# Sliding-window attention ahead of two expert layers: two-bank score tiles, one maximum per chunk and a shorter list of weight conversions

## The chip, the cores and the metric

The program runs on one core of a Trainium2 chip. The metric is the device time of one execution in microseconds (us); the profile's own clock starts with the first instruction (the span). The engines are called TensorE (PE in the rows, its weight loads PEld), VectorE (DVE), ScalarE (ACT), GpSimd (POOL) and SyncE (SP, which only issues DMAs).

## The reference

```python
scores = (1 / sqrt(64)) * q @ k.T            # 4 batches, 8 heads, 576 positions, head size 64
scores = where(0 <= i - j < 64, scores, -1e9)
attn = softmax(scores); x = attn @ v         # x: 2304 tokens x 512
logits = x @ w_gate                          # 8 experts
# every (token, expert) pair in falling order of its logit: give the token to the expert
# if the token has none yet and the expert has fewer than 288
out[e's tokens] = relu(x[e's tokens] @ w1[e]) @ w2[e]        # 512 -> 1024 -> 512
h = out @ w_in; y = maximum(0.01 * h, h) @ w_out             # 512 -> 2048 -> 512
```

## The kernel before

There are three stages in one program, and each engine works its own list of instructions in the order of the program text.

**Attention** (`attention`, lines 58 to 223) handles 18 chunks of 128 queries, two windows of 64 each; a query looks at two windows of keys. For chunk c, `scores` writes a mask and then 32 small matmuls into score tiles; VectorE takes the maximum per query and head (line 131) and multiplies it by -0.125 (line 133); `exps` makes four exponentials on ScalarE for either half a of the heads (line 139), with that number as bias. `trans` turns the probabilities with eight matmuls into the PSUM tile "apt", and ScalarE copies each half out (line 146). `values` makes 32 matmuls into the tile "ao"; VectorE adds up, inverts, forms the logits (the values carry eight more columns for them) and scales the rows (line 169, tile "ax"), which a DMA writes to "xd". The loop runs one chunk ahead for scores and two behind for values: scores(i), exps(i,0), values(i-2), trans(i-1), exps(i,1), then `filler`, then the gate stages, then the loads that fall due.

The extra columns of the values come from `stage_g` (eight matmuls, v times the gate weights, for three chunks at a time, tile "ag", copied by ScalarE at line 95) and, one chunk later, `stage_gt` (twelve small matmuls that turn it, tile "ag" again, copied by VectorE at line 108; then five copies on GpSimd make the shifted values "ave"). They stand at the end of chunks 0, 2, 5, 8, 11, 14 and of the chunk after each.

PSUM has eight banks for it: three score tiles of one bank ("as"), one for "ag", two for "apt", two for "ao".

`filler` is called twice a chunk. It runs steps of the router that can go ahead (`Router.ahead`) and steps of `Convert`: the weights of the last layer come as 32 packed units, and each is opened by two operations on ScalarE (lines 574 and 576), put together by two on VectorE (589 and 597), and for the first twelve split into a rounded high part (a cast, line 599) and a remainder (a subtraction, line 582), both on GpSimd as long as attention runs (`self.side`). Up to CVA = 9 units are done inside attention, from chunk 5 on.

**The router** (`Router.phase`, one phase per expert) is a long chain of small VectorE operations and small matmuls. Phase 0 runs alone after attention; the later ones, and the conversion of the other units, are cut into steps that `RouteDriver.tick` strews between the matmuls of the **expert layers** (`Moe.run`), by a planner that keeps estimated clocks of the engines (`Clocks`). In `tick`, conversion steps go ahead of router steps while fewer units are done than a goal that grows with the step number; `R.finish(m)` at a fixed step runs what is left of phase m at once. All of their operations carry line 1050.

Of the kernel before, what the change touches and what calls it, by code (L numbers as in the profile page):

```python
# [57 lines left out]
NC = 18  # L58
def attention(nc, tc, ident, identb, qT, kT, v, vT, wg_sb, maskb, xd, L, filler, early, late, done):


    with ExitStack() as ctx:
# [25 lines left out]
        gate = {}  # L88
        def stage_g(m):

            ps = pp.tile([128, 384], F32, tag="ag", name=f"ag{m}", bufs=1)
            for u in range(4):
                nc.tensor.matmul(ps[32 * u:32 * u + 32, :], wg_sb[:, u, :], vtb[m][:, u, :], start=True, stop=True, skip_group_check=True)
            gate[m] = wk.tile([128, 384], F32, tag="agb", name=f"agb{m}", bufs=1)
            nc.scalar.copy(gate[m], ps)
            ve[m] = big.tile([128, 3, 8, VW], F32, tag="ave", name=f"ave{m}", bufs=NV)
            if m % 3:
                nc.gpsimd.tensor_copy(ve[m][64:128, 0], vo[m - 1][64:128, 2])
            else:
                nc.gpsimd.memset(ve[m][64:128, 0], 0.0)  # L100
        def stage_gt(m):
            gs = gate.pop(m)
            pt = pp.tile([128, 3, 8, 8], F32, tag="ag", name=f"agt{m}", bufs=1)
            pick = ident.rearrange("p (h e) -> p h e", h=8)[:, :, :8]
            for j in range(6):
                h = 64 * (j % 2)
                nc.tensor.matmul(pt[h:h + 64, j // 2], gs[:, 64 * j:64 * j + 64], pick, start=True, stop=True, skip_group_check=True)
            nc.vector.tensor_copy(vo[m][:, :, :, 64:72], pt)
            for j in range(3):
                nc.gpsimd.tensor_copy(ve[m][0:64, j], vo[m][0:64, j])  # L110
                if j < 2:
                    nc.gpsimd.tensor_copy(ve[m][64:128, j + 1], vo[m][64:128, j])
        ss, ps_, ts = {}, {}, {}
        def scores(c):
            kind = 1 if c % 9 == 0 else 2 if c % 9 == 4 else 0
            mk = maskb[:, 128 * kind:128 * kind + 128].unsqueeze(1).to_broadcast([128, 4, 128])
            S = [pp.tile([128, 4, 128], F32, tag="as", name=f"as{c}_{a}", bufs=3) for a in range(2)]
            for a in range(2):
                nc.tensor.matmul(S[a], identb, mk, start=True, stop=False, skip_group_check=True)
            for u in range(4):  # L120
                for t in range(2):
                    b, w = divmod(2 * c + t, 9)
                    pos = KPOS[b % 2]
                    x, y = sorted((pos[w], pos[w - 1]))
                    q, k = qb[(2 * c + t) // 3][:, 4 * (w % 3) + u], kb[b][:, x:y + 1:y - x, u, :]
                    for a in range(2):
                        h = slice(64 * a, 64 * a + 64)
                        nc.tensor.matmul(S[a][64 * t:64 * t + 64, u, :].rearrange("p (b c) -> p b c", b=2), q[h], k[h], start=False, stop=True, skip_group_check=True)
            for a in range(2):
                mx = wk.tile([128, 4], F32, tag=f"amx{a}", name=f"amx{c}_{a}")  # L130
                nc.vector.tensor_reduce(out=mx, in_=S[a], axis=AX.X, op=ALU.max)
                nm = wk.tile([128, 4], F32, tag=f"anm{a}", name=f"anm{c}_{a}")
                nc.vector.tensor_scalar(out=nm, in0=mx, scalar1=-0.125, scalar2=None, op0=ALU.mult)  # L133
                ss[c, a] = S[a], nm
        def exps(c, a):
            S, nm = ss.pop((c, a))
            p = ps_[c, a] = wk.tile([128, 4, 128], F32, tag="ap", name=f"ap{c}_{a}", bufs=4)
            for u in range(4):
                nc.scalar.activation(p[:, u, :], S[:, u, :], AF.Exp, bias=nm[:, u:u + 1], scale=0.125)  # L139
        def trans(c, a):  # L140
            p = ps_.pop((c, a))
            pt = pp.tile([128, 4, 128], F32, tag="apt", name=f"apt{c}_{a}", bufs=2)
# [2 lines left out]
            ts[c, a] = wk.tile([128, 4, 128], F32, tag="aptb", name=f"aptb{c}_{a}", bufs=4)  # L145
            nc.scalar.copy(ts[c, a], pt)
        def values(c):
            O = pp.tile([128, 2, 512], F32, tag="ao", name=f"ao{c}", bufs=1)
            o = O[:, :, :4 * VW].rearrange("p g (h e) -> p g h e", e=VW)
            m, s = divmod(c, 3)  # L150
            for a in range(2):
                ptb = ts.pop((c, a))
                for u in range(4):
                    h = 2 * u + a
                    for t in range(2):
                        nc.tensor.matmul(o[64 * t:64 * t + 64, h // 4, h % 4, :], ptb[:, u, 64 * t:64 * t + 64], (ve, vo)[t][m][:, s, h, :], start=True, stop=True, skip_group_check=True)
# [8 lines left out]
            if c == NC - 1:  # L165

                done(c)
            x = wk.tile([128, 512], F32, tag="ax", name=f"ax{c}", bufs=2)
            nc.vector.tensor_tensor(out=x.rearrange("p (g h d) -> p g h d", g=2, h=4), in0=o[:, :, :, 0:64], in1=r4.to_broadcast([128, 2, 4, 64]), op=ALU.mult)
            nc.sync.dma_start(xd[128 * c:128 * c + 128, :], x)  # L170
            if c < NC - 1:
                done(c)
        due = {}
        def at(i, f, *a):
            due.setdefault(max(i, -1), []).append((f, a))
# [5 lines left out]
        for m in range(NV, 6):  # L181
            at(3 * (m - NV) + 4, load_v, m)
        for m in range(2, 6):
            at(max(3 * (m - 2) - 1, 0), load_vt, m)
# [15 lines left out]
        for part in range(3):  # L200
            load_k(1, part)
        load_v(2)
        for i in range(NC + 2):
            if i < NC:
                scores(i)
                exps(i, 0)
# [5 lines left out]
            if i < NC:  # L212
                exps(i, 1)
            for h in range(2):
                filler(2 * i + h)
            for m in range(6):
                if i == max(3 * m - 1, 0):
                    stage_g(m)
                if i == max(3 * m - 1, 0) + 1:
# [323 lines left out]
class Convert:  # L543
# [5 lines left out]
    def __init__(self, nc, pool, wio, res):  # L549
        self.nc, self.pool, self.wio, self.res = nc, pool, wio, res  # L550
        self.st, self.nl, self.done, self.g, self.ng, self.hold = {}, 0, 0, None, None, False
        self.side = nc.gpsimd.tensor_copy, nc.gpsimd
        self.out, self.taken, self.due, self.came, self.now = {}, set(range(NRES)), None, {}, lambda: 0
    def load(self, eng=None):
        n = self.nl
# [421 lines left out]
                self.ystep(i)  # L977


CVA, CV0, CVL, CVX = 9, 8, 3, (2, 1, 1)  # L980
class Clocks:


# [137 lines left out]
def build(nc, tc, qT, kT, v, vT, wg, cfd, cid, cbd, w12, wio, out):  # L1121
    with ExitStack() as ctx:
# [18 lines left out]
        cvp = ctx.enter_context(tc.tile_pool(name="cvp", bufs=1))  # L1141
        cv = Convert(nc, cvp, wio, res)
        def filler(i):
            if queue and not next(queue[0], False):
# [4 lines left out]
            if CV0 + 2 <= i < 35:  # L1149
                for _ in range(CVX[i % 3]):  # L1150
                    if cv.done < CVA:
                        cv.piece()
        rp = ctx.enter_context(tc.tile_pool(name="rp", bufs=1))
        rt = Router(nc, rp, None, L, cf, ci, cb, ones, make_pow2(nc, rp))
        ahead = {5: (0, 6), 11: (6, 12), 14: (12, 15), 17: (15, 18)}
        queue = []
        def done(c):
            if c in ahead:
                queue.append(rt.ahead(*ahead[c]))
            if c == NT - 1:  # L1160
                for g in queue:
                    list(g)
# [47 lines left out]
```

## Time and profile before

| | us |
|---|---|
| median of 3 runs | 827.08 |
| lowest and highest run | 824.98, 829.12 |
| the profiled execution | 835.9 |
| its span | 834.2 |
| TensorE busy in it | 771.0 |
| VectorE busy | 472.3 |
| ScalarE busy | 310.7 |
| GpSimd busy | 144.5 |

The profile is of one execution. A row of a timeline gives start, length, engine, line, operation and the tile written and read; the brackets name an idle time ahead of it and what ended that. Matmuls overlap, so the pitch from one start to the next says more than a length.

### The profile page before, as it was taken

The page shows a single profiled execution, that of the slowest core. Times are in us where ns is not written, and L with a number is a line of the kernel's source. Part 1 is how long each engine was busy: PE and PEld are TensorE (multiplying, and loading weights), DVE is VectorE, ACT ScalarE, POOL GpSimd, SP SyncE. Part 2 cuts the span into 40 slices and gives each one's busy share as a digit, 9 for nine tenths or more (in the row PEclk, how much of TensorE's full clock was granted, in tenths as well). Part 3 has the DMA queues.
Part 4 walks back from the last instruction along what each step waited for, and adds up shares of the span by engine and source line. Part 5 has one row for each costly group of instructions (what it writes and reads, how often), then busy time and mean ns, then how long its engine had stood idle before and what let it go on. Part 6 is the DMA issues. An engine that isn't in the chain of part 4 may idle for free.

```text
span 834.2 us, 15155 instructions
## 1 busy us (share of the span) xinstructions
PE 771.0 (92%) x5829; PEld 639.4 (77%) x5829; DVE 472.3 (57%) x1271; ACT 310.7 (37%) x692; POOL 144.5 (17%) x173
## 2 busy tenths in 40 slices
PE   5878844999999999999999998999999999999996
PEld 3656632679878778998777787988888998888896
DVE  3698878489767878878585782322224213222332
ACT  4787721035227644532111233522224442211322
POOL 2256302010010002101000034710004661000200
PEclk9999965999999999999999998999999999999999
DMA  9997324358027977636132446563343945323652
GB/s 352 388 413 257 102 76 142 115 160 211 13 78 271 311 277 160 154 95 207 51 127 83 146 138 128 124 224 101 112 167 108 214 99 193 99 101 129 235 191 102
DMA packets 44728, 138.70 MB, mean 166 GB/s; under 512 B 9712, under 2 KB 10608, under 8 KB 44656
## 3 DMA queue, kind: packets, MB, share of 16 engines
q1 hardware_dynamic: 40816, 126.36, 46.8%
q0 software_dynamic: 3408, 11.01, 4.4%
q8 instruction: 46, 0.75, 0.4%
q10 hardware_dynamic: 432, 0.36, 0.1%
q14 instruction: 26, 0.21, 0.1%
HBM read 117.78 MB, written 19.93 MB: 165 GB/s over the span
## 4 chain that ended last, share of the span: by engine, by line
PE 51%; issue 5%; DVE 5%; DMA 4%; ACT 1%; POOL 1%; another core or an unknown queue 1%; POOLq 0%; ACTq 0%; DVEq 0%; SPq 0%
PE h L1050 24%; PE oa L1050 18%; PE ya L1050 6%; PE rp L1050 2%; DMA raw<-in_w_dram 1%; DMA xg<-xd,r_ids 1%; DVE r_ob L1050 1%; DMA cv_in<-in_wio_dram 1%; DVE w L1050 1%; PE xtp L1050 1%; DMA sidx<-idl 1%; POOL w L1050 1%; ACT w L1050 0%; DMA out_dram<-ot,sidx 0%
## 5 line engine op out<-in xcount | busy, mean ns | idle before, releaser
L1050 PE MATMUL h<-Y,w 128*128 128x512 f32 (+1 forms) x600 | 137.9, 375 | 0.0
L1050 PE MATMUL oa<-w,hh 128*128 128x512 f32 x540 | 134.0, 393 | 0.0
L1050 DVE SCALAR_TENSOR_TENSOR h<-h,tg 128x512 f32<-128x512 f32 (+1 forms) x80 | 51.6, 645 | 130.2 <-ACT tg L1050 127.9
L1050 ACT COPY tg<-h 128x512 f32<-128x512 f32 (+1 forms) x80 | 43.5, 544 | 211.8 <-PE h L1050 211.3
L1050 PEld LDWEIGHTS h<-Y,w 128*128 128x128 f32 x600 | 104.3, 188 | 20.4
L1050 PEld LDWEIGHTS oa<-w,hh 128*128 128x128 f32 x540 | 99.8, 188 | 20.8
L1050 PE MATMUL ya<-hh,w 128*128 128x288 f32 x672 | 102.5, 299 | 0.7 <-ACT hh L1050 0.7
L1050 PE MATMUL h<-xT,w 128*128 128x288 f32 x672 | 101.8, 299 | 0.0
L1050 PEld LDWEIGHTS h<-xT,w 128*128 128x128 f32 x672 | 93.4, 190 | 1.1 <-issue 0.2
L1050 PEld LDWEIGHTS ya<-hh,w 128*128 128x128 f32 x672 | 93.1, 190 | 1.2 <-ACT hh L1050 0.9
L1050 PE MATMUL oa<-res,hh 128*128 128x512 f32 x324 | 84.0, 399 | 0.0
L1050 PE MATMUL h<-Y,res 128*128 128x512 f32 (+1 forms) x360 | 83.0, 373 | 0.0
L1050 POOL TENSOR_TENSOR w<-raw,w 128x512 fp32r<-128x512 f32 x45 | 56.7, 1290 | 119.2 <-ACT w L1050 119.2
L1050 ACT ACTIVATE hh<-h 128x288 fp32r<-128x288 f32 (+1 forms) x64 | 26.3, 411 | 130.4 <-PE h L1050 117.2
L1050 POOL DMA_INDIRECT out_dram<-ot,sidx x18 | 17.9, 994 | 326.7 <-DVE ot L1050 220.3
L1050 DVE TENSOR_TENSOR hh<-h,hh 128x512 fp32r<-128x512 f32 (+1 forms) x80 | 51.0, 637 | 37.3 <-ACT hh L1050 35.5
L1050 PEld LDWEIGHTS h<-Y,res 128*128 128x128 f32 x360 | 62.3, 188 | 11.8
L1050 PEld LDWEIGHTS oa<-res,hh 128*128 128x128 f32 x324 | 59.2, 188 | 13.1
L1050 ACT CAST hh<-h 128x512 fp32r<-128x512 f32 (+1 forms) x80 | 43.5, 544 | 64.0 <-DVE h L1050 61.2
L1050 ACT CAST w<-raw 128x512 fp32r<-128x512 f32 x112 | 63.9, 618 | 7.7 <-DMA raw<-in_w_dram 7.7
L1050 DVE SCALAR_TENSOR_TENSOR hh<-h,hh 128x288 fp32r<-128x288 f32 x56 | 25.5, 455 | 63.5 <-ACT hh L1050 60.8
L139 ACT ACTIVATE ap<-as,anm 128x128 f32<-128x128 f32 x144 | 41.8, 391 | 26.8 <-DVE anm L133 24.3
(153 smaller groups left out, 942.0 us busy)
## 6 DMA issues: line engine op xcount, KB each, us to landing
w<-wsp SPq DMA_DIRECT2D x80, 512.0 KB, 4.6
raw<-in_w_dram SPq DMA_DIRECT2D x61, 512.0 KB, 6.3
cv_in<-in_wio_dram SPq DMA_DIRECT2D x32, 512.0 KB, 5.5
wsp<-w SPq DMA_DIRECT2D x20, 512.0 KB, 3.5
avo<-in_v_dram SPq DMA_DIRECT2D x6, 876.0 KB, 10.2
aq<-in_q_dram SPq DMA_DIRECT2D x12, 384.0 KB, 7.2
avt<-in_vt_dram SPq DMA_DIRECT2D x6, 768.0 KB, 10.9
xd<-ax SPq DMA_DIRECT2D x18, 256.0 KB, 7.0
```

What stands on the lines that cost most here:

```text
L139: nc.scalar.activation(p[:, u, :], S[:, u, :], AF.Exp, bias=nm[:, u:u + 1], scale=0.125)
L1050: return f(*a, **kw)
```

## The change

- The score tile is one tile of two banks for a chunk, and there are two of them ("as", bufs=2). One VectorE instruction takes the maximum over both halves; the multiplication by -0.125 moves to ScalarE, as a copy with a scale (`negate`), ahead of the exponentials.
- "ag" is gone: `stage_g` and `stage_gt` take tiles of "apt".
- The first gate stage moves from the end of chunk 0 into chunk 1, and the loads of vt and q, k are issued in another order.
- The loop ends with chunk 16; the work on the last two chunks is written out by hand. `values` of these two write into score tiles. `values` returns its scaling of the rows as a function, so that it can be placed after the logits of a later chunk.
- `Convert`'s cast goes to ScalarE and its subtraction to VectorE inside attention too. CVA is 6. The router's steps ahead for chunks 15 to 17 are cut in two.

```diff
-            S = [pp.tile([128, 4, 128], F32, tag="as", name=f"as{c}_{a}", bufs=3) for a in range(2)]
+            S = pp.tile([128, 2, 4, 128], F32, tag="as", name=f"as{c}", bufs=2)
...
-            for a in range(2):
-                mx = wk.tile([128, 4], F32, tag=f"amx{a}", name=f"amx{c}_{a}")
-                nc.vector.tensor_reduce(out=mx, in_=S[a], axis=AX.X, op=ALU.max)
-                nm = wk.tile([128, 4], F32, tag=f"anm{a}", name=f"anm{c}_{a}")
-                nc.vector.tensor_scalar(out=nm, in0=mx, scalar1=-0.125, scalar2=None, op0=ALU.mult)
-                ss[c, a] = S[a], nm
+            mx = wk.tile([128, 2, 4], F32, tag="amx", name=f"amx{c}")
+            nc.vector.tensor_reduce(out=mx, in_=S, axis=AX.X, op=ALU.max)
+            ss[c] = S, mx
+        def negate(c):
+            S, mx = ss[c]
+            nm = wk.tile([128, 2, 4], F32, tag="anm", name=f"anm{c}")
+            nc.scalar.activation(nm, mx, AF.Copy, scale=-0.125)
+            ss[c] = S, nm
...
-            ps = pp.tile([128, 384], F32, tag="ag", name=f"ag{m}", bufs=1)
+            ps = pp.tile([128, 384], F32, tag="apt", name=f"ag{m}", bufs=2)
...
-            pt = pp.tile([128, 3, 8, 8], F32, tag="ag", name=f"agt{m}", bufs=1)
+            pt = pp.tile([128, 3, 8, 8], F32, tag="apt", name=f"agt{m}", bufs=2)
...
-            O = pp.tile([128, 2, 512], F32, tag="ao", name=f"ao{c}", bufs=1)
+            if c < NC - 2:
+                O = pp.tile([128, 2, 512], F32, tag="ao", name=f"ao{c}", bufs=1)
+            else:
+                O = pp.tile([128, 2, 4, 128], F32, tag="as", name=f"ao{c}", bufs=2).rearrange("p g h e -> p g (h e)")
...
-        load_vt(0)
         load_q(1)
         load_k(0, 1)
+        load_vt(0)
         load_v(0)
...
+        for i in range(NC - 1):
+            scores(i)
+            negate(i)
+            exps(i, 0)
+            if i == 1:
+                stage_g(0)
             if i >= 2:
-                values(i - 2)
-            if 1 <= i <= NC:
+                values(i - 2)()
+            if i >= 1:
                 trans(i - 1, 0)
                 trans(i - 1, 1)
-            if i < NC:
-                exps(i, 1)
+            exps(i, 1)
+            if i == 1:
+                stage_gt(0)
...
+        y, z = NC - 2, NC - 1
+        scores(z)
+        trans(y, 0)
+        trans(y, 1)
+        negate(z)
+        exps(z, 0)
+        exps(z, 1)
+        n0 = values(y - 1)
+        n1 = values(y)
+        filler(None)
+        n0()
+        trans(z, 0)
+        trans(z, 1)
+        n2 = values(z)
+        n1()
+        n2()
...
-        self.side = nc.gpsimd.tensor_copy, nc.gpsimd
+        self.side = nc.scalar.copy, nc.vector
...
-CVA, CV0, CVL, CVX = 9, 8, 3, (2, 1, 1)
+CVA, CV0, CVL, CVX = 6, 8, 3, (2, 1, 1)
...
-        ahead = {5: (0, 6), 11: (6, 12), 14: (12, 15), 17: (15, 18)}
+        ahead = {5: (0, 6), 11: (6, 12), 14: (12, 15), 16: (15, 17), 17: (17, 18)}
```

## Rows read from the trace of the kernel before

**Rows 1.** Stretches: length, busy us (instructions) per engine, granted clock, DMA share, GB/s.

```profile
20.00:60.00 40.00, 33.62 (x643) 24.67 (x640) 31.71 (x85) 32.13 (x91) 14.58 (x21) 1.00 1.01 401
60.00:110.00 50.00, 36.77 (x638) 28.18 (x637) 42.13 (x112) 33.14 (x95) 22.23 (x27) 0.92 0.49 175
...
146.00:230.00 84.00, 82.61 (x618) 65.67 (x618) 63.44 (x207) 26.48 (x59) 3.26 (x4) 0.98 0.44 124
230.00:340.00 110.00, 109.67 (x643) 89.94 (x643) 86.91 (x200) 56.46 (x104) 9.75 (x14) 1.00 0.69 211
```

**Rows 2.** Groups by line, 0 to 110 us: busy, mean ns | idle before, releasers.

```profile
L131 DVE TENSOR_REDUCE amx<-as 128x4 f32<-128x512 f32 x36 | 24.6, 684 | 6.7 <-PE as L128 6.4
...
L119 PE MATMUL as<-maskb,cbt 128*128 128x512 bf16 x36 | 13.4, 400 | 20.1 <-ACT ap L139 13.0 <-DMA cbt<-in_cb_dram 6.1 <-DVE asm L158 1.0
...
L133 DVE TENSOR_SCALAR anm<-amx 128x4 f32<-128x4 f32 x36 | 11.3, 313 | 2.1
```

**Rows 3.** Timeline of TensorE, chunks 5 and 6: start, length, line, tiles, idle before.

```profile
34.05 0.85 PE L93 MATMUL ag<-avt,wg_sb 128*32 128x384 f32 x8
34.84 0.60 PE L119 MATMUL as<-maskb,cbt 128*128 128x512 bf16 x2
35.37 1.10 PE L128 MATMUL as<-ak,aq 64*64 64x128 f32 x32
36.41 0.28 PE L156 MATMUL ao<-ave,aptb 128*64 128x73 f32 x1
...
37.57 1.09 PE L144 MATMUL apt<-cft,ap 128*128 128x128 f32 x8
39.38 0.57 PE L107 MATMUL agt<-cft,agb 128*64 128x64 f32 x12 [0.72 <-ACT agb L95]
```

**Rows 4.** Timeline of ScalarE: its first instruction, and chunk 3.

```profile
2.17 0.20 ACT L1135 ACTIVATE cft<-ones 128x1 f32<-128x1 bf16 x1
...
23.00 1.14 ACT L139 ACTIVATE ap<-as,anm 128x128 f32<-128x128 f32 x4 [0.75 <-DVE anm L133]
24.01 1.09 ACT L146 COPY aptb<-apt 128x512 f32<-128x512 f32 x2
24.95 0.42 ACT L139 ACTIVATE ap<-as,anm 128x128 f32<-128x128 f32 x1
```

**Rows 5.** Timelines of VectorE (two scalings) and GpSimd (one subtraction).

```profile
45.42 0.17 DVE L133 TENSOR_SCALAR anm<-amx 128x4 f32<-128x4 f32 x1
...
60.28 0.95 DVE L133 TENSOR_SCALAR anm<-amx 128x4 f32<-128x4 f32 x1
...
59.93 1.27 POOL L582 TENSOR_TENSOR res<-cv_r,res 128x512 fp32r<-128x512 f32 x1
```

**Rows 6.** Timelines of VectorE and ScalarE: two waits of the conversion.

```profile
37.67 0.69 DVE L589 SCALAR_TENSOR_TENSOR cv_r<-cv_r,cv_in 128x512 int32<-128x512 int32 x1 [2.39 <-ACT cv_in L576]
...
67.27 0.66 ACT L574 ACTIVATE cv_r<-cv_in 128x512 f32<-128x512 f32 x1 [2.78 <-DMA cv_in<-in_wio_dram]
```

**Rows 7.** Timelines: ScalarE's first copies of chunks 1 and 14; end of attention.

```profile
19.74 0.60 ACT L146 COPY aptb<-apt 128x512 f32<-128x512 f32 x1
...
92.96 1.09 ACT L146 COPY aptb<-apt 128x512 f32<-128x512 f32 x2
...
107.82 0.27 DVE L164 TENSOR_REDUCE L<-al 128x8 f32<-128x64 f32 x1
...
109.23 0.68 DVE L169 TENSOR_TENSOR ax<-ao,ari 128x512 f32<-128x512 f32 x1
...
109.97 1.13 PE L1050 MATMUL rp<-r_oh,r_ge 128*63 128x8 bf16 x18 [2.88 <-DVE ax L169]
```

**Rows 8.** After attention: ScalarE's casts (groups), phase 3's list, a gather (timelines).

```profile
L1050 ACT CAST res<-cv_r 128x512 fp32r<-128x512 f32 x3 | 1.9, 617 | 25.2 <-DVE cv_r L1050 25.2
...
333.56 0.16 DVE L1050 CAST r_ids<-rp 96x3 int32<-96x3 f32 x1 [0.52 <-PE rp L1050]
...
346.13 0.52 PE L1050 MATMUL xtp<-cft,xg 96*128 96x96 f32 x4 [0.87 <-DMA xg<-xd,r_ids]
```

More of the change, by code (lines that the diff above doesn't have):

```diff
@@ L116, in scores @@
             mk = maskb[:, 128 * kind:128 * kind + 128].unsqueeze(1).to_broadcast([128, 4, 128])
-            S = [pp.tile([128, 4, 128], F32, tag="as", name=f"as{c}_{a}", bufs=3) for a in range(2)]
+            S = pp.tile([128, 2, 4, 128], F32, tag="as", name=f"as{c}", bufs=2)
             for a in range(2):
-                nc.tensor.matmul(S[a], identb, mk, start=True, stop=False, skip_group_check=True)
+                nc.tensor.matmul(S[:, a], identb, mk, start=True, stop=False, skip_group_check=True)
             for u in range(4):
@@ L127, in scores @@
                         h = slice(64 * a, 64 * a + 64)
-                        nc.tensor.matmul(S[a][64 * t:64 * t + 64, u, :].rearrange("p (b c) -> p b c", b=2), q[h], k[h], start=False, stop=True, skip_group_check=True)
-            for a in range(2):
-                mx = wk.tile([128, 4], F32, tag=f"amx{a}", name=f"amx{c}_{a}")
-                nc.vector.tensor_reduce(out=mx, in_=S[a], axis=AX.X, op=ALU.max)
-                nm = wk.tile([128, 4], F32, tag=f"anm{a}", name=f"anm{c}_{a}")
-                nc.vector.tensor_scalar(out=nm, in0=mx, scalar1=-0.125, scalar2=None, op0=ALU.mult)
-                ss[c, a] = S[a], nm
+                        nc.tensor.matmul(S[64 * t:64 * t + 64, a, u, :].rearrange("p (b c) -> p b c", b=2), q[h], k[h], start=False, stop=True, skip_group_check=True)
+            mx = wk.tile([128, 2, 4], F32, tag="amx", name=f"amx{c}")
[6 more added lines that the diff above has]
+            ss[c] = S, nm
         def exps(c, a):
-            S, nm = ss.pop((c, a))
+            S, nm = ss[c]
             p = ps_[c, a] = wk.tile([128, 4, 128], F32, tag="ap", name=f"ap{c}_{a}", bufs=4)
             for u in range(4):
-                nc.scalar.activation(p[:, u, :], S[:, u, :], AF.Exp, bias=nm[:, u:u + 1], scale=0.125)
+                nc.scalar.activation(p[:, u, :], S[:, a, u, :], AF.Exp, bias=nm[:, a, u:u + 1], scale=0.125)
         def trans(c, a):
@@ L164, in values, with norm @@
             nc.vector.tensor_reduce(out=L[:, c, :], in_=l.rearrange("p h e -> p e h"), axis=AX.X, op=ALU.add)
[L165 to L172, printed above, removed]
+            done(c)
+            def norm():
+                x = wk.tile([128, 512], F32, tag="ax", name=f"ax{c}", bufs=2)
+                nc.vector.tensor_tensor(out=x.rearrange("p (g h d) -> p g h d", g=2, h=4), in0=o[:, :, :, 0:64], in1=r4.to_broadcast([128, 2, 4, 64]), op=ALU.mult)
+                nc.sync.dma_start(xd[128 * c:128 * c + 128, :], x)
+            return norm
         due = {}
@@ L202, in attention @@
         load_v(2)
-        for i in range(NC + 2):
-            if i < NC:
-                scores(i)
-                exps(i, 0)
+        for i in range(NC - 1):
[4 more added lines that the diff above has]
+                stage_g(0)
             if i >= 2:
-                values(i - 2)
-            if 1 <= i <= NC:
+                values(i - 2)()
+            if i >= 1:
                 trans(i - 1, 0)
                 trans(i - 1, 1)
-            if i < NC:
-                exps(i, 1)
+            exps(i, 1)
+            if i == 1:
+                stage_gt(0)
             for h in range(2):
                 filler(2 * i + h)
-            for m in range(6):
-                if i == max(3 * m - 1, 0):
+            for m in range(1, 6):
+                if i == 3 * m - 1:
                     stage_g(m)
-                if i == max(3 * m - 1, 0) + 1:
+                if i == 3 * m:
                     stage_gt(m)
@@ L1143, in filler @@
         def filler(i):
+            if i is None:
+                drain()
+                return
             if queue and not next(queue[0], False):
@@ L1148, in filler @@
                     cv.load()
-            if CV0 + 2 <= i < 35:
+            if CV0 + 2 <= i < 32:
                 for _ in range(CVX[i % 3]):
@@ L1160, in done, with drain @@
             if c == NT - 1:
-                for g in queue:
-                    list(g)
+                drain()
+        def drain():
+            while queue:
+                list(queue.pop(0))
         with tc.tile_pool(name="mk", bufs=1) as mk:
```

2 lines of the change are left out of this document (1 added, 1 removed).

## The prediction

> **What bounds the kernel now.** I read the page first, then the stretches, then inside attention the groups by line, and last the timelines of single engines, for pitches (start to next start). In [rows 1] the reader is to see two kernels in one. From 146 us on TensorE is busy practically all the time (82.6 of 84 us from 146 to 230, 109.7 of 110 from 230 to 340): what VectorE, ScalarE and GpSimd do there costs nothing unless a matmul has to wait for it. Before that no engine is full: TensorE has 33.6 of 40 us from 20 to 60 and 36.8 of 50 from 60 to 110, where VectorE has 42.1. So the change is worth what it moves the end of attention, the first router matmul at 109.97 us [rows 7], plus what it does to the waits of the later stages.
>
> From 20 to 60 us the DMA engines are full as well (share 1.01, 401 GB/s). Inside attention the groups [rows 2] name the wait: TensorE's mask matmuls idled 13.0 us for the exponentials. That is the loop of before: with three score banks the second half of chunk c+1 needs the bank of exps(c,0).
>
> **What the change adds: a new loop.** The eight PSUM banks are dealt anew: two score tiles of two banks each, two banks for "apt", two for "ao". Scores of the next chunk no longer wait for this chunk's exponentials. But the gate product (stage_g, chunks 2, 5, 8, 11, 14) and its transpose (stage_gt, one chunk later) lose their own bank and take a slot of "apt". There the oldest tile is trans(i-1,0), and it is free only when ScalarE has copied it, which it does after exps(i,0). TensorE executes in order, so scores(i+1), queued behind the gate product, waits for that too, and behind it reduce(i+1) on VectorE and negate(i+1) on ScalarE. I count from the end of one first copy to the end of the next.
>
> Pieces: gate product 0.79 (34.05 to 34.84), two masks 0.53, scores 1.10 to their end or 1.04 to the next start, values 1.16, gate transpose 0.57 [rows 3]; four exponentials 1.01, two copies 0.94, the first of them ended after 0.60 [rows 4, 7]; a hand-over between engines 0.06 (109.91 to 109.97, [rows 7]). The transposes of a chunk take 1.09 by their row, 1.03 to the next start with the overlap that the scores show. Not shown before are two operations. The maximum over 1024 elements lies between 0.68 (one half, as now) and 1.37 (both halves one after the other); from 0.27 for 64 elements [rows 7] and 0.684 for 512 [rows 2] the slope is 0.93 ns an element, which gives 1.16; I take 1.22, since the small one does not read PSUM. The negation on ScalarE lies between 0.17 (VectorE's undisturbed, [rows 5]) and 0.60 (a copy of 512, [rows 7]); the nearest row is its 128x1 activation, 0.20 [rows 4]; with the wait behind it I take 0.25.
>
> - Chunk with a gate product: 0.06+0.79+0.53+1.10+0.06+1.22+0.06+0.25+1.01+0.60 = 5.68.
> - Chunk with a gate transpose: the same with 0.57 for 0.79, 5.46.
> - Third chunk: nothing in the ring, so TensorE's own work, 0.53+1.04+1.16+1.03 = 3.76. In chunks that also convert a weight unit, ScalarE's: 0.25+1.01+0.94+1.01, an opening of two operations of 0.66 with the same overlap, 1.26, and the cast that comes from GpSimd 0.62 [rows 6, 8], together 5.1.
>
> **The sum for attention.** From the first copy of chunk 2 (end 20.34) to that of chunk 15 (end 93.56) the kernel before takes 73.2 us [rows 7]. After: five gate products 28.4, four gate transposes 21.8, third chunks 3.76+5.1+5.1+3.76 = 17.7, together 67.9: 5.3 less. Against that stand two stalls that my count does not hold and that the change leaves in place. At the first unit VectorE waits 2.39 us for the opening on ScalarE with the next maximum queued behind it; now the cast is queued ahead of the negation as well; I charge 1.5. And the opening of unit 6 waits 2.78 us for its DMA, issued into the full queues [rows 6]; that load is asked for at the same chunk again; between 0 and 2.8, I charge 0 to 1.9. The start loses 0.8: stage_g(0) now stands in chunk 1, and transposing the second half of chunk 0 waits for its slot. The tail, from the last first copy to the router: gate transpose and scores(16) 2.2; maximum, negation 1.6; then ScalarE without a break, exponentials and copies of 16 and copies of 15, 4.4; negation and exponentials of 17, 2.3; transpose, copy and values of the last half 2.0; the values' small operations up to the logits, four like the one in [rows 7], 1.0; the router's six 1.1 (108.09 to 109.23); and two normalisations instead of one, since both now stand behind the logits, 1.3. That is 15.9 against 16.4 before: 0.5 won. In all 1.6 to 3.5 us won; I take 2.5.
>
> What lies beside: VectorE is busy 0.84 of the time from 60 to 110 [rows 1], some 4.7 us of a chunk of 5.6 (73.2 over 13). The change takes two scalings of 0.31 mean and half a maximum's start from that and adds 0.9 of a subtraction of about 0.69 in a converting chunk. So its part stays near 4.7 us of 5.1 to 5.7: covered, with under 1 us to spare. The moved vt and gate loads go to the same SP queue in another order; chunk 1 needs k and q first and gets them first: nothing. Fewer conversions in attention ask for three loads less of 512 KB by its end: nothing, since the queues are at 0.49 by then [rows 1].
>
> [Rows 5] show why the scaling leaves VectorE: this one, 0.17 us when alone, took 0.95 and ended with GpSimd's subtraction. Over 36 of them that is 11.3 - 36 x 0.17 = 5.2 us [rows 2]. In my ring VectorE has slack, so none of it is in the sum. The Trainium skill (SBUF — State Buffer, "Who interferes with whom") has a rule for it: a VectorE operation in a two-port mode and a GpSimd one exclude each other for the whole instruction, and a VectorE operation with two SBUF inputs also excludes GpSimd reads. By it the 5.2 us vanish, but the subtraction that moves to VectorE reads two SBUF tiles and still meets GpSimd's value copies. If VectorE and not the ring sets the pace, up to those 5.2 us would come on top of my 2.5; this is the second rival's case.
>
> **What is moved out.** Units 6, 7 and 8 are converted after attention: three steps of 0.69 each, 6.2 us of VectorE, and 3 x (1.26+0.62) = 5.6 us of ScalarE [rows 6, 8]. From 146 to 230 VectorE has 63.4 of 84 us and TensorE 82.6 [rows 1]: I cost them at nothing. The cover is VectorE's idle 20 us there. If it is gone, the router's later rounds slip behind the conversions.
>
> On the profiled execution (span 834.2, time 835.9) the sum gives 833.4. The measured runs have a median of 827.08; the 2.5 us lie in a stretch of 110 us and aren't scaled: 824.6.
>
> **Rivals.** First, the forecast: attention ends 2.5 us earlier (1 to 4), the rest follows unchanged, 823 to 826.
>
> Second, faster: the gate's stages don't close the ring, because the chain of a whole chunk has a slot free when they come, or VectorE's disturbed operations were what set the pace. Without the ring three chunks cost 3 x 3.76 + 0.79 + 0.57 = 12.6 for 14.9 without conversion, and 3 x 5.1 = 15.3 and a gate copy for 16.2 with it; four such triples make some 5 us more, 819.6. The disturbed scalings give about the same. For it: VectorE is the busiest engine from 60 to 110. Against: the slot's owner is plain in the code.
>
> Third, slower: the three units collide with the router. The expert after next needs its token list at a fixed place in the order; phase 3's list is written at 333.56 and the gather that follows is already waited for, 0.87 us at 346.13 [rows 8]. There is no slack. If the 6.2 us push that phase back, TensorE waits for most of it: 4 to 6 us, less 0 to 2.5 from attention: 829 to 833. It decides from the point where the list lands over 1 us later in TensorE's order than now. For it: 333.56 is just in time, and conversions go ahead of router steps. Against: VectorE has 23 of 110 us idle from 230 to 340.
>
> Fourth, nothing arrives: full DMA queues up to chunk 11 hold every faster chunk back, 827.
>
> **How the numbers follow.** Forecast 0.38, faster rival 0.32, slower rival 0.22, DMA 0.08. Half a per cent, about what can be told from no change, is 4.1 us: below 822.9 or above 831.2. The faster rival and a corner of the forecast lie below, 0.35; of the slower rival and other mishaps above 831.2 there is 0.2; the rest 0.45. The range goes from 815 (ring and disturbances both gone, 2.5 + 5 + 5) to 832.
>
> **What would show it.** In the changed profile: the maximum 128x1024 at 1.16 to 1.37; the negation near 0.2; TensorE idle for a ScalarE copy ahead of each gate product and transpose, about 1 us each, and no longer ahead of the masks; first copies 5.7, 5.5 and 3.8 us apart, or 5.7, 5.5 and 5.1 where units are converted; the first router matmul near 107.5; phase 3's list and the wait for its gather. I am wrong if gate stages start without that wait, if the list comes late against TensorE's work, or if TensorE's granted clock falls below its 0.92 of 60 to 110 us because its waits become longer.

## The result, and the profile after

The changed kernel takes 834.61 us (median of 20 runs, 831.16 to 839.51), the kernel before 829.85 on the same chip (20 runs, 824.98 to 832.35): ratio 1.0059, 95% interval 1.0041 to 1.0076, so 4.9 us slower (3.4 to 6.3). The forecast was 824.6, with a range up to 832. It was counted from 827.08, the median of three runs of before; with 829.85 for 20 runs, 2.8 of the 10.0 us by which it missed are the base, and the rest is a change that loses where it was to win 2.5.

The two profiles side by side hide this. The profiled execution of after (span 833.0, time 834.6) lies at its median; that of before (span 834.2, time 835.9) lies 6 us above its own, and two more profiles of before took 834.95 and 833.67. So differences of totals below come from the runs without a profile, and the profiles are used stretch by stretch.

Stretches of the changed kernel, columns as in [rows 1]:

```profile
20.00:60.00 40.00, 30.82 (x580) 22.38 (x580) 27.68 (x63) 33.70 (x99) 8.70 (x14) 1.00 1.00 393
60.00:110.00 50.00, 39.20 (x718) 29.41 (x717) 33.09 (x92) 34.31 (x104) 12.11 (x17) 0.93 0.39 149
146.00:230.00 84.00, 82.97 (x616) 66.85 (x615) 66.82 (x206) 31.30 (x68) 2.84 (x3) 0.99 0.57 140
230.00:340.00 110.00, 108.57 (x656) 89.52 (x653) 88.36 (x205) 56.37 (x106) 11.01 (x14) 1.00 0.69 214
```

The change does relieve VectorE: 33.1 us from 60 to 110 instead of 42.1 (the units moved out are part of that). It brings nothing, because VectorE is no longer what the next maximum waits for. The groups by line of attention (0 to 110 us) show for what:

```profile
L119 PE MATMUL as<-maskb,cbt 128*128 128x512 bf16 x36 | 12.1, 422 | 6.0 <-DMA cbt<-in_cb_dram 6.0
L93 PE MATMUL ag<-avt,wg_sb 128*32 128x384 f32 x48 | 5.8, 556 | 9.5 <-ACT aptb L148 9.5
L107 PE MATMUL agt<-cft,agb 128*64 128x64 f32 x72 | 3.4, 230 | 5.2 <-ACT aptb L148 5.2
...
L135 ACT ACTIVATE anm<-amx 128x8 f32<-128x8 f32 x18 | 3.8, 209 | 27.1 <-DVE amx L130 26.9
...
L130 DVE TENSOR_REDUCE amx<-as 128x8 f32<-128x1024 f32 x18 | 22.0, 1223 | 19.1 <-PE as L128 17.7 <-ACT aptb L148 1.4
```

The masks' wait for exponentials (13.0 us in [rows 2]) is gone, as the change intends. In its place the gate product waits 9.5 us and the gate transpose 5.2 us for ScalarE's copy of the transposed probabilities. One turn of that loop, from the timelines of ScalarE, TensorE and VectorE (start, length):

```profile
26.03 1.09 ACT L148 COPY aptb<-apt 128x512 f32<-128x512 f32 x2
...
26.68 0.57 PE L107 MATMUL agt<-cft,agb 128*64 128x64 f32 x12 [1.12 <-ACT aptb L148]
27.18 0.60 PE L119 MATMUL as<-maskb,cbt 128*128 128x512 bf16 x2
27.72 1.10 PE L128 MATMUL as<-ak,aq 64*64 64x128 f32 x32
...
28.99 1.22 DVE L130 TENSOR_REDUCE amx<-as 128x8 f32<-128x1024 f32 x1 [1.33 <-PE as L128]
...
30.24 0.21 ACT L135 ACTIVATE anm<-amx 128x8 f32<-128x8 f32 x1 [2.08 <-DVE amx L130]
30.48 1.14 ACT L141 ACTIVATE ap<-as,anm 128x128 f32<-128x128 f32 x4
31.50 1.09 ACT L148 COPY aptb<-apt 128x512 f32<-128x512 f32 x2
```

Each line starts within 0.2 us of the end of the one above (the copy's first half ends at 26.63): from copy to copy 5.47 us in which the engines work one after the other. Attention ends where it ended before, the first router matmul at 109.53 against 109.97 [rows 7]:

```profile
109.53 0.32 PE L1072 MATMUL rp<-r_oh,r_ge 128*63 128x8 bf16 x5 [3.95 <-DVE ax L173]
```

Behind attention one thing differs most. Phase 3's list is written at 333.95, when before wrote it too (333.56 [rows 8]), but TensorE is further in its order. Timelines of VectorE, GpSimd and TensorE:

```profile
333.95 0.16 DVE L1072 CAST r_ids<-rp 96x3 int32<-96x3 f32 x1 [0.42 <-PE rp L1072]
...
334.38 1.17 POOL L1072 DMA_INDIRECT xg<-xd,r_ids  x1 [11.22 <-DVE r_ids L1072]
...
345.34 0.55 PE L1072 MATMUL xtp<-cft,xg 96*128 96x96 f32 x4 [3.31 <-DMA xg<-xd,r_ids]
347.40 0.87 PE L1072 MATMUL xtp<-cft,xg 96*128 96x96 f32 x4 [1.51 <-DMA xg<-xd,r_ids]
347.97 3.23 PE L1072 MATMUL ya<-hh,w 128*128 128x288 f32 x12
```

TensorE asks for the gathered rows at 342.03 (345.34 - 3.31), 8.1 us after the list; in before at 345.26, 11.7 us after it. They come 11.4 us after the list here, 12.6 us there. So before waited 0.87 us and the changed kernel 3.31 and 1.51. These waits cost more than their length: the twelve matmuls behind them take 3.23 us where before has 1.82 (at 346.43), and TensorE's granted clock is 0.80 from 340 to 350 us and 0.86 from 350 to 360, where before has 1.00 in both.

### The profile page after: what moved, and what is told of

Read it like the earlier page. It is cut to its first block, busy times and chain, and to the rows that moved or that the text cites. A ratio compares the mean times of both kernels' runs of the same rounds, so it can differ in the third digit from the quotient of the medians.

```text
span 833.0 us, 15078 instructions
## 1 busy us (share of the span) xinstructions
PE 769.0 (92%) x5828; PEld 638.0 (77%) x5829; DVE 467.1 (56%) x1239; ACT 318.6 (38%) x719; POOL 120.7 (14%) x148
## 4 chain that ended last, share of the span: by engine, by line
PE 71%; DVE 11%; DMA 7%; issue 5%; ACT 4%; POOL 0%; POOLq 0%; ACTq 0%; SPq 0%; DVEq 0%
PE h L1072 32%; PE oa L1072 21%; PE ya L1072 10%; PE rp L1072 4%; ACT ap L141 2%; DMA xg<-xd,r_ids 2%; DVE amx L130 2%; DMA raw<-in_w_dram 2%; DMA xd<-ax 1%; PE as L128 1%; DVE r_ob L1072 1%; PE xtp L1072 1%; DVE w L1072 1%; DMA cft<-in_cf_dram 1%; ACT aptb L148 1%
## 5 line engine op out<-in xcount | busy, mean ns | idle before, releaser
L1072 PE MATMUL h<-Y,res 128*128 128x512 f32 (+1 forms) x360 | 81.1, 371 | 0.0
L1072 POOL DMA_INDIRECT out_dram<-ot,sidx x18 | 19.9, 1106 | 308.9 <-DMA w<-wsp 93.5
L1072 POOL TENSOR_TENSOR w<-raw,w 128x512 fp32r<-128x512 f32 x37 | 46.6, 1288 | 122.1 <-ACT w L1072 101.6
L1072 DVE TENSOR_TENSOR w<-raw,w 128x512 fp32r<-128x512 f32 x75 | 49.3, 697 | 3.2 <-ACT w L1072 2.9
```

Source lines behind the costliest of these rows:

```text
L1072: return f(*a, **kw)
```

## The experiments

Differences to before are ratio minus one, times 830, each against runs of before on the same chip; their intervals are about plus or minus 1.5 to 3 us. Where two rows are compared below, these differences are subtracted and not the medians, since the chips differ ("by ratio").

| run | whole, us (ratio, interval) | to before | first router matmul (profile) |
|---|---|---|---|
| changed | 834.61 (1.0059, 1.0041-1.0076) | +4.9 | 109.5, 108.1 |
| changed, nine units | 838.72 (1.0079, 1.0051-1.0108) | +6.6 | 115.4 |
| before, six units | 831.29 (1.0011, 0.9983-1.0038) | +0.9 | 102.3 |
| changed, gate behind scores | 829.40 (0.9979, 0.9956-1.0003) | -1.7 | 102.7 |
| before, new banks only | 841.87 (1.0130, 1.0098-1.0161) | +10.8 | 121.5 |
| changed, GpSimd converts | 835.48 (1.0057, 1.0035-1.0079) | +4.7 | 107.9 |
| gate behind scores, FORCE 5 | 823.12 (0.9907, 0.9877-0.9938) | -7.7 | 101.3 |
| changed, FORCE 5 | 832.78 (1.0023, 0.9999-1.0048) | +1.9 | 109.3 |
| gate behind scores, nine units | 827.90 (0.9983, 0.9962-1.0004) | -1.4 | 107.4 |

The first theory was the third rival: attention is as good as before, and the moved units cost the time behind it.

**The units put back, and the units moved alone.** In the changed kernel:

```diff
-CVA, CV0, CVL, CVX = 6, 8, 3, (2, 1, 1)
+CVA, CV0, CVL, CVX = 9, 8, 3, (2, 1, 1)
-            if CV0 + 2 <= i < 32:
+            if CV0 + 2 <= i < 35:
```

and the reverse in the kernel before. Behind attention each then issues its instructions in the other kernel's order.

> The changed kernel with one part undone: units 6, 7 and 8 are converted in attention again (9 units, up to the last chunk), so that everything behind attention is issued in the order of the kernel before; attention itself stays as changed. Theory A (the moved units cost the time, in the stages behind attention): the stretch from expert 2's start to expert 4's start falls back from about 72.7 us (the changed kernel) to about 64.5 (before), attention ends 0 to 2 us later than in the changed kernel (109.5) because three units more lie in it; in all 828 to 832, at or below the kernel before (829.9). Theory B (attention's new ring and its waits cost the time, the order behind it is as good): 834 to 838, the first router matmul 1 to 4 us later than 109.97 and the stages behind unchanged in length.

> The kernel before with that one part done: only six units are converted in attention, three behind it, so that everything behind attention is issued in the changed kernel's order. Theory A: attention ends 0 to 1.5 us earlier than 109.97, the stretch from expert 2's start to expert 4's start takes about 72 us instead of 64.5, TensorE waits 3 to 5 us for a gather of phase 3 there; in all 833 to 837. Theory B: 828 to 831, no change.

Measured: 838.72 and 831.29. Theory A's totals fail in both: putting the units back makes it slower, and moving them alone costs nearly nothing. Theory B's ranges are missed too, though narrowly (838.72 for 834 to 838, 831.29 for 828 to 831), and attention moved by more than either theory said: 115.4 for the router's first matmul with the units put back, 102.3 with them moved out. The profile of the second run shows what the sum had missed. With six units and the old banks, attention is 7 us shorter (ScalarE's copies, as in [rows 7], and the router's first matmul):

```profile
19.76 0.60 ACT L146 COPY aptb<-apt 128x512 f32<-128x512 f32 x1
...
85.62 0.60 ACT L146 COPY aptb<-apt 128x512 f32<-128x512 f32 x1
...
102.34 0.42 PE L1050 MATMUL rp<-r_oh,r_ge 128*63 128x8 bf16 x8 [2.87 <-DVE ax L169]
```

From the first of these copies to the second the kernel before takes 73.2 us, with six units 65.9; the changed kernel, with six units too, 72.6. The removal of three units alone wins 7.3 us there, and the rest of the change gives them back. And theory A's stretch holds too. What the expectations call expert 2's start to expert 4's start runs from 313.2 to 385.8 us in the changed kernel, 72.7 us with the wait for the gather; it takes 73.4 us in this run, against 64.3 in before (66.9 and 67.4 in its other two profiles) and 69.0 in the changed kernel with nine units.

**Second profiles.**

> The kernel before, unchanged, for a second profile of it, since the one shown is 6 us over the median of its runs. If the stretch from expert 4's start on (64.4 us with a 3.9 us wait for the router) was the unlucky part of that profile, it takes about 60.5 here and the time is about 829 to 831; the router's first matmul stays at 109.5 to 110.5.

> The changed kernel, unchanged, for a second profile. Theory A: the waits for phase 3's gather, 3.3 and 1.5 us near 346 us in the first profile, stand here too (3 to 6 us together), and the stretch from expert 2 to expert 4 takes 71 to 74 us again. If they are absent here and the time is about the same, theory A falls.

> The kernel before, unchanged, for one more profile. Two profiled executions took 834.95 and 835.9 us where its runs without a profile have a median near 829.5. If the spread is in attention (TensorE's granted clock 0.90 and 0.92 of 60 to 110 us in those two), a profile near 830 shows a clock of 0.95 or more there and the first router matmul at 105 to 107; if it is elsewhere, the router starts at 110 again and a later stretch is shorter.

Before: 834.95 and 833.67, router at 111.2 and 109.6; the wait of 3.88 us near 504 us in the first profile is 0.7 in both, so it belongs to that execution alone, and taking it out did not bring the time down to the 829 to 831 expected. The clock of 60 to 110 us is 0.90 and 0.93. Neither profile lies near 830, so what the shorter runs do differently was not caught. After: 835.76, gather waits of 3.2 and 1.0 us again, 72.2 us for that stretch. The late gather is no accident of one profile.

**The ring broken.** Gate product and transpose move from the end of their chunk to behind its scores. The slot that they take is then that of a half copied a chunk earlier:

```diff
             scores(i)
+            for m in range(1, 6):
+                if i == 3 * m - 1:
+                    stage_g(m)
+                if i == 3 * m:
+                    stage_gt(m)
             negate(i)
...
-            for m in range(1, 6):
...
```

> The changed kernel with the gate product and the gate transpose of expert pairs 1 to 5 issued right behind the scores of their chunk, ahead of the values, instead of at the chunk's end: the slot that they take is then that of a half copied a chunk earlier, and the next scores no longer queue behind a copy that follows this chunk's exponentials. Theory ring (the loop through the shared slot is what the change pays with): TensorE's idle time ahead of gate product and transpose (9.5 and 5.2 us in the changed kernel) goes, chunks of 5.7 and 5.5 us fall to about 4 to 5, the last first copy of attention but three (chunk 14's) at 84 to 89 us instead of 91.4 to 92.9, and the whole takes 826 to 831. Rival (ScalarE, with the scaling, the casts and the copies, sets the pace by itself): pitches stay over 5.3 us, ScalarE's idle time does not fall, 833 to 836.

Measured: 829.40, by ratio 6.6 us below the changed kernel, router at 102.73. The groups of attention in this run:

```profile
L93 PE MATMUL ag<-avt,wg_sb 128*32 128x384 f32 x48 | 5.1, 500 | 3.0 <-ACT aptb L148 3.0
L107 PE MATMUL agt<-cft,agb 128*64 128x64 f32 x72 | 4.1, 261 | 0.0
...
102.73 0.22 PE L1072 MATMUL rp<-r_oh,r_ge 128*63 128x8 bf16 x1 [3.96 <-DVE ax L173]
```

The waits fall from 14.7 to 3.0 us (what is left stands at 47.60 and 64.25, in two chunks that convert), and undisturbed chunks take 4.4, 4.0 and 3.7 us where the ring took 5.7, 5.5 and 3.6. In these ScalarE does not set the pace by itself; the seven from the first conversion on still take 4.7 to 7.3. Part of the waiting only moves: the transposes of the probabilities now wait 7.2 us in all instead of 2.6, 4.3 of it for ScalarE's copy of the gate product. The ring theory holds. But from the copy of chunk 1 to that of chunk 14 this loop takes 65.6 us (21.94 to 87.50), and the old one with six units took 65.9: without the ring the new loop is as good as the old one, not better.

**The banks alone**, in the kernel before:

```diff
-            ps = pp.tile([128, 384], F32, tag="ag", name=f"ag{m}", bufs=1)
+            ps = pp.tile([128, 384], F32, tag="apt", name=f"ag{m}", bufs=2)
-            pt = pp.tile([128, 3, 8, 8], F32, tag="ag", name=f"agt{m}", bufs=1)
+            pt = pp.tile([128, 3, 8, 8], F32, tag="apt", name=f"agt{m}", bufs=2)
-            S = [pp.tile([128, 4, 128], F32, tag="as", name=f"as{c}_{a}", bufs=3) for a in range(2)]
+            S2 = pp.tile([128, 2, 4, 128], F32, tag="as", name=f"as{c}", bufs=2)
+            S = [S2[:, 0], S2[:, 1]]
```

> The kernel before with the banks dealt as in the change and nothing else: two score tiles of two banks, the gate's product and transpose in the slots of the transposed probabilities; two half maxima, their scaling on VectorE, conversion on GpSimd, nine units and the order of the tail as before. Theory ring: the same loop closes here, with 0.68 of a half maximum and 0.31 of a scaling in the place of 1.22 and 0.25, so 5.3 us for a chunk with a gate product and 5.0 with a transpose against 4.3 to 4.9 before; chunks that convert stay at 6 to 7; attention 1 to 4 us longer, 831 to 835. Rival (the ring is only the price of the long maximum, its banks alone gain): masks no longer wait for exponentials (13 us idle go), 825 to 829.

Measured: 841.87, 10.8 us slower than before, more than expected. Timelines of VectorE and ScalarE in chunk 3:

```profile
26.85 0.69 DVE L132 TENSOR_REDUCE amx<-as 128x4 f32<-128x512 f32 x1 [2.54 <-PE as L129]
27.64 0.17 DVE L134 TENSOR_SCALAR anm<-amx 128x4 f32<-128x4 f32 x1
27.72 0.68 DVE L132 TENSOR_REDUCE amx<-as 128x4 f32<-128x512 f32 x1
28.51 0.17 DVE L134 TENSOR_SCALAR anm<-amx 128x4 f32<-128x4 f32 x1
...
28.52 1.14 ACT L140 ACTIVATE ap<-as,anm 128x128 f32<-128x128 f32 x4 [2.33 <-DVE amx L132]
```

The first exponentials start at 28.52, after the second half's maximum, not after the first scaling at 27.81: with both halves in one tile they waited for both. So the loop holds both maxima and takes 5.8 and 5.6 us, and chunks that also convert up to 7.7. Some 4 us go at the start, where the first gate stage still stands in chunk 0: the copy of chunk 1 starts at 23.70 instead of 19.74 (20.30 in the changed kernel). So the banks are the costly part of the change. That the other parts (the later first gate stage, one maximum, scaling on ScalarE) soften it fits the changed kernel with nine units, +6.6, but no run takes them one by one.

**Conversions back on GpSimd**, the rest as changed:

```diff
-        self.side = nc.scalar.copy, nc.vector
+        self.side = nc.gpsimd.tensor_copy, nc.gpsimd
```

> The changed kernel with the conversion's cast and subtraction back on GpSimd in attention; the rest as changed. Theory ring, ScalarE inside it: in the five converting chunks 0.62 of a cast leaves ScalarE, whose chain is the ring, and 0.69 of a subtraction leaves VectorE, which has slack: those chunks shorten by up to 0.6 us, 1 to 3 us less in all, 831.5 to 833.5. Rival (VectorE's and GpSimd's operations disturb each other): the maxima and VectorE's own steps lengthen beside GpSimd's subtraction by some tenths of a us each, no gain or 1 to 3 us more, 834 to 838.

Measured: 835.48, the same as the changed kernel within the intervals; router at 107.87, 0.2 to 1.7 us earlier. The gain of 1 to 3 us did not come, and the total lies in the rival's range; that GpSimd's disturbance ate the gain was not shown. Which engine casts and subtracts matters too little to be told apart here.

**Attention alone.** All cut in the same way:

```diff
-        rt.pp = ctx.enter_context(tc.tile_pool(name="rps", bufs=1, space=PSUM))
...
-        m.run()
+        nc.sync.dma_start(out[0:128, 0:NT * 8], L.rearrange("p c e -> p (c e)"))
```

> The kernel before cut off behind attention: the router's rounds, the experts and the output are left out (only the logits are written out at the end). What is asked: whether attention takes in an execution without a profile what the profile shows. Three profiled executions of before took 833.7 to 835.9 us, its runs without a profile 829.4 to 830.7 by median; the profiles of the changed kernel (834.6, 835.8) agree with its runs (834.6). Theory P (the profile lengthens attention of the kernel before, with its nine units and GpSimd's operations): without a profile this is 4 to 6 us shorter than profiled, and 3 to 5 us shorter than the changed kernel's attention alone. Theory Q (attention is as the profiles show, the difference lies behind it): profiled and other runs agree within 1.5 us and this takes 0 to 2.5 us longer than the changed kernel's attention (110.0, 111.2 and 109.6 against 109.5 and 108.1 for the first router matmul).

> The changed kernel cut off behind attention in the same way (router rounds, experts and output left out). Theory P: 3 to 5 us longer than the cut kernel before in runs without a profile, its own profile within 1.5 us of them. Theory Q: 0 to 2.5 us shorter than the cut kernel before.

> The kernel before with six units in attention, cut off behind attention in the same way. The profile put its first router matmul at 102.3, 7 to 9 us before that of before with nine. Theory P: without a profile the three units cost only 0 to 3 us here, so this is 0 to 3 us shorter than the cut kernel before. Theory Q: 7 to 9 us shorter, and 5.5 to 7 us shorter than the changed kernel's attention.

> The changed kernel with gate product and transpose right behind the scores, cut off behind attention in the same way. Its profile put the first router matmul at 102.7, 5.4 to 6.8 us before the changed kernel's; the whole was 5.2 us shorter. Both theories: 4.5 to 7 us shorter than the changed kernel's attention alone; if it is less than 3, part of that gain came from behind attention.

Measured, medians of 5 or 6: before 114.31 (112.86 to 116.82), changed 115.46 (114.73 to 119.35), before with six units 108.95, gate behind scores 108.67. The profiled executions (112.86, 115.57, 109.11, 107.63) lie within 1.5 us of these and none above by more than 0.2, so theory P falls. Theory Q misses too in part: before was to take 0 to 2.5 us longer than the changed kernel and takes 1.1 less, and the six units were to win 7 to 9 and win 5.4. The ledger of attention: units moved out -5.4, the rest of the change +6.5, together +1.1; with so few runs each is known to about 2 us. Breaking the ring gives 6.8 back, which accounts for its 6.6 us in the whole kernel.

So of the 4.9 us lost, 1.1 arise in attention and 3.8 behind it. In the same way, before with six units has 0.9 + 5.4 = 6.3 us more behind attention, and the gate behind scores -1.7 + 5.6 = 3.9: all three with six units.

**The late list.** Between phase 3's list and the transposes that need its rows, TensorE's order has 94 matmuls with nine units, 60 with six, and 103 with six and FORCE 5 (the expectation below counts four more in each). FORCE is how many steps ahead of an expert `R.finish` runs what is left of its phase:

```diff
-FORCE, LEAD = 4, 10
+FORCE, LEAD = 5, 10
```

> The changed kernel with gate product and transpose right behind the scores (as in the run that broke the ring) and, behind attention, the router's phases finished one step earlier (FORCE 5 instead of 4), so that 107 matmuls instead of 64 lie between the list of phase 3 and the transposes that need its gathered rows. Theory late list (the third rival: six units in attention push phase 3's list and gather late against TensorE, 4 to 7 us of waits near 345 us): those waits fall below 1.5 us, the stretch from the router's first matmul to the end falls from 725.6 to 721 to 723, in all 825 to 827, 3 to 5 us below the kernel before. Rival (the stages behind attention lose to the conversions themselves, VectorE's work): the wait moves to the list's own matmuls, in all 828.5 to 830.5.

> The changed kernel with that one step alone (FORCE 5 instead of 4), attention as changed. Theory late list: the waits for phase 3's gather (3.3 and 1.5 us, 3.2 and 1.0) go, 3 to 5 us less in all, 830 to 831.5; what is left over the kernel before is attention's ring. Rival: 833.5 to 835.

> The changed kernel with gate product and transpose right behind the scores and nine units converted in attention again, so that everything behind attention is issued in the order of the kernel before. What is asked: the price of the three units in attention where the ring is broken, and whether order or attention makes the difference behind it. Theory late list: behind attention 722 to 724 us from the router's first matmul (as in the kernel before) instead of 725.6; attention 4 to 7 us longer than 102.7; in all 829 to 832. Rival (the stretch behind attention depends on when it starts, not on the units): 725 or more behind attention, 833 to 836 in all.

The transposes of 300 to 360 us in the changed kernel, with the gate behind the scores, and with FORCE 5 as well (groups):

```profile
L1072 PE MATMUL xtp<-cft,xg 96*128 96x96 f32 x16 | 2.8, 314 | 4.8 <-DMA xg<-xd,r_ids 4.8
```

```profile
L1072 PE MATMUL xtp<-cft,xg 96*128 96x96 f32 x16 | 2.9, 325 | 5.7 <-DMA xg<-xd,r_ids 5.7
L1072 PE MATMUL rp<-r_ob,r_rhs 128*6 128x96 bf16 x18 | 1.1, 205 | 0.7 <-DVE r_ob L1072 0.7
```

```profile
L1072 PE MATMUL xtp<-cft,xg 96*128 96x96 f32 x12 | 1.3, 246 | 0.0
L1072 PE MATMUL rp<-r_ob,r_rhs 128*6 128x96 bf16 x18 | 1.1, 206 | 2.2 <-DVE r_ob L1072 2.2
```

The wait is gone; 1.5 of 5.7 us come back as a longer wait for the list's own operations, and the clock falls behind that one too (the next twelve matmuls, at 325.08, take 3.25 us instead of 1.75). The whole takes 823.12, 7.7 us below before and 12.6 (by ratio) below the changed kernel: faster than both. It was expected at 825 to 827. In the changed kernel alone FORCE 5 gives 832.78, 3.0 us by ratio, where 3 to 5 were expected; its median lies above the 831.5 that was written. Behind attention that leaves 1.9 - 1.1 = 0.8 us over before. With nine units and the ring broken, 827.90, below the 829 to 832 expected: no wait for the gather either, and 716.8 us from the router's first matmul to the end, less than the 722 to 724 expected.

Two limits. FORCE 5 moves the lists of phases 3 to 7, not only phase 3's, though no wait for a gather stands behind 360 us with it or without it. And the kernel before was not run with FORCE 5: it too waits 0.9 to 2.2 us for phase 3's gather in its three profiles, so how much it would win is open, and the 7.7 us below before are not the worth of the change.

## Why the prediction was wrong

**The ring: mechanism and size right.** Chunks of 5.73, 5.47 and 3.63 us stand where 5.68, 5.46 and 3.76 were worked out, the maximum takes 1.22 as taken, the negation 0.21 with the exponentials 0.24 after its start (0.25). TensorE waits ahead of gate product and transpose and no longer ahead of the masks. The start lost 0.56 (0.8), and the tail, from the copy of chunk 14 to the router, won 0.35 (0.5). The second rival, that the ring does not close, fell.

**First failed step: "5.3 less".** The 67.9 us of the changed loop were compared with 73.2 of before, nine units included. But with six units before takes 65.9. The difference that I credited to the new loop was the three units' going, and the loop itself was already a loss of 2.0 by my own sum (3.5 to 5.4 with the two stalls that I charged apart), 6.7 by measurement. No term priced the old loop with six units; its timeline had the rows for it (chunks without conversion 4.0 to 5.0 us apart).

**Second: the converting chunks were mis-sized.** 67.9, 1.5 for the first stall and 0 to 1.9 for the last opening make 69.4 to 71.3; measured 72.6, and 71.2 in the second profile. So the second profile is inside what was charged and the first 1.3 above it. The first conversion came out as charged (7.13 for 5.68 + 1.5), and the last opening waited 0.2 us for its DMA, so nothing of its charge was needed. What took its place are three chunks, in the first profile 6.05 for 5.46, 5.80 for 5.1 and 7.62 for 5.68: 3.2 us. In the first two the maximum comes late, as here in the second, VectorE:

```profile
65.55 1.16 DVE L611 SCALAR_TENSOR_TENSOR cv_r<-cv_r,cv_in 128x512 int32<-128x512 int32 x1
67.29 0.69 DVE L604 TENSOR_TENSOR res<-cv_r,res 128x512 fp32r<-128x512 f32 x1 [0.57 <-ACT res L621]
67.90 1.22 DVE L130 TENSOR_REDUCE amx<-as 128x8 f32<-128x1024 f32 x1
```

The scores ended at 65.01; the maximum starts 2.9 us later, behind the subtraction that now stands on VectorE and waits for ScalarE's cast. "Covered, with under 1 us to spare" counted busy time only and not this order. The third chunk starts behind the wait of 3.49 us that this delay leaves on TensorE, and its 1.9 us are the clock's (below): gate product, masks and scores take 4.4 us instead of 2.4.

**Third: "I cost them at nothing".** The moved units cost 3.8 us behind attention (+4.9 less +1.1, known to about 2 us; 6.3 where they alone were moved). The third rival had the place, the mechanism and the price (4 to 6 us): phase 3's list, late against TensorE's order by more than 1 us, here 8.1 instead of 11.7 us ahead of its use. As a difference, 1.5 to 6 us over before, it holds the measured 4.9; its 829 to 833 lies too low by the 2.8 us of the base. It let attention win 0 to 2.5, though, where attention lost 1.1. The argument against it, VectorE's idle 23 us, does not bear on it: the order places the list and its use, and neither idle time nor busy time shows how far apart they stand. The FORCE 5 runs show that the place in the order is the cause: with it 3.0 of the 3.8 us come back. That the units are what shifts it follows from the five profiles with six units and FORCE 4, which all have the wait (3.3 to 5.7 us), against 0.0 to 2.3 in six with nine units.

**Clock.** It fell as feared, but in places: after a wait of 3.49 us, up to 71.06, the scores took 1.99 instead of 1.10 us, and the granted clock from 71.0 to 76.2 us is 0.50, the lower of its two levels:

```profile
71.06 1.51 PE L93 MATMUL ag<-avt,wg_sb 128*32 128x384 f32 x8 [3.49 <-ACT aptb L148]
72.50 1.03 PE L119 MATMUL as<-maskb,cbt 128*128 128x512 bf16 x2
73.46 1.99 PE L128 MATMUL as<-ak,aq 64*64 64x128 f32 x32
```

That chunk took 7.62 us, and 6.53 in the second profile, where gate product and masks still ran at full speed. From 60 to 110 us the granted clock is 0.93, though, no lower than the 0.92 of before; so the sign that the prediction named did not come, and with the ring broken it is 0.87 in a shorter run.

**VectorE against GpSimd.** The rule of the Trainium skill (SBUF — State Buffer, "Who interferes with whom") had 5.2 us vanish with the scaling. The scaling's lengthening is gone from VectorE, but the time does not show it: inside the ring VectorE waits 17.7 us for scores. The rule's second half, two SBUF inputs against GpSimd's reads, agrees with the trace of the changed kernel: the putting-together at 65.55 (above) takes 1.16 us, 0.68 at 59.38 while GpSimd is idle, and GpSimd's value copy beside it, at 65.13, 1.03 instead of 0.67. No run here tests the rule by itself.

**Open.** The three profiles of before lie 3 to 6 us above its median of other runs; the runs of attention alone show that this does not arise there, but where it does was not found. From the router's first matmul to the end, the nine-unit order took between 716.8 and 724.2 us in six profiles, the six-unit order 723.5 to 726.4 in five. The waits for phase 3's gather, 0.0 to 2.3 us in the six, are too small for their spread of 7.4, which stays unexplained. The 3.0 us of FORCE 5 in the changed kernel and the 6.0 with the ring broken differ, but each is known only to about 3 us; behind attention the profiles have 3 to 6 and 4.

## What to carry to other kernels

When a change both removes work and rearranges the rest, price the old arrangement with that work removed, and compare the new one with that; otherwise the removal hides a loss. A buffer that is saved by sharing has to be followed in program order: ask who frees the slot, and what else is queued behind the one that waits for it; here five lines moved to another place in the loop won back 6.6 us. Where an order is fixed ahead, measure the distance from a result to its use, not the idle time around it.

## What was not expected of the hardware

Two executions of the same kernel differ by up to 10 us, and TensorE's clock goes with it: of 20 runs of before, the shortest (826.27 us) had a mean granted clock of 0.976, the longest (835.86) 0.968; the correlation of the time with the time spent at the lower of the two levels is 0.76 in that set, and 0.49 to 0.79 in three other sets of before. In the changed kernel the three gathers of phase 3 landed 10.9 to 11.4 us after their issue, while all 24 gathers had a median of 4.4 and the transfers of 512 KB of conversions one of 5.9; what held these back was not found.
